# Even and odd dims of a head, gate and value weights in two loads, and an instruction order that is charged for changes of product kind

## The chip, the cores and the metric

The kernel runs on one core of a Trainium2 chip. The metric is device time in microseconds (us) of one execution. The profile is that of one execution; its span runs from the first to the last instruction of the program.

## The reference

Softcap attention, then a gated MLP, then a cosine MLP, all in float32 (the MLP weights come as float64):

```python
scores = cap * tanh((q @ k.T) / sqrt(64) / cap)       # 4 batches, 12 heads, 448 x 448
attn = exp(scores - max) / (sum + 1e-9);  o = attn @ v
x = o.transpose(0, 2, 1, 3).reshape(1792, 768)
y = (sigmoid(x @ w_gate) * (x @ w_val)) @ w_out        # 768 -> 1536 -> 768
h = y @ w_in2;  out = (h * cos(h)) @ w_out2            # 768 -> 2048 -> 768
```

## The kernel before, in words

**Planner.** The program is written by generators ("threads"), each of which yields one operation at a time (`Op`) with its engine, a cost in us, and what it reads and writes. `Order.run` (L184) keeps a planned time for each engine and, again and again, emits the thread whose operation can start earliest, after a penalty that the thread carries (L207). The order that comes out on each engine is the program; nothing is reordered on the chip. So a cost or a penalty changes no work, only the order. Two threads feed TensorE: `on_pe` of the attention, whose own sequence is fixed (L1535), and `whole` (L1770), which makes all other products. Until the key "late" is set they have penalties `ATT_PEN` (0.0) and `A_PEN` (0.5); after it `ATT_PE2` (0.5) and `A_PEN` (0.5), until the attention's last scores are out. "late" is set when the attention reaches step `W_FROM` (L1542); a step is half a group, and it also lets the loads of the gate and value weights begin (L563).

**Attention.** 12 groups of 4 heads of one batch; groups 0 to 5 make the first half of the tokens (x0), 6 to 11 the second (x1). A group has 8 scores steps (L1453: 2 heads at once, 6 matmuls of 448 columns over 64 rows), 8 values steps (L1482: 4 heads at once, each into its own 32 columns of the array; one step makes 32 of the 64 dims of each head), one step of sums (L1510, the same shape as a values step), and 4 transposes steps (L1429). ScalarE makes tanh and exp of every scores step. The reciprocal and the division (L1715, L1736) are VectorE's. Tiles of probabilities (`p`) lie in the 5 big buffers, as long as more than `P_BIG` are free, else in two small ones. They are freed by the values steps.

**Gate and value, first half.** 24 units of 128 columns of `w_gate` and `w_val`. A unit is loaded as raw float64 into a big buffer (`raw_load`, L438), converted to float32 by bit operations (`convert`: two on ScalarE, four on VectorE), kept in HBM for the second half (L493), split into a high and a low part (L519 ScalarE, L530 VectorE or GpSimd), and used for 6 product steps of 6 matmuls of 448 columns (L744). The rows of x0 in tile 2j + s are dims s * 32 to s * 32 + 31 of the four heads of group j, so a unit's rows are gathered by 8 transfers of 32 partitions (4 heads by 2 halves, `by_heads`, L413). At most one raw unit is on its way while the attention runs, two after. The units of the cosine MLP are loaded and converted in the background, one each `BG_STEP` us of the plan from `BG_FROM` on.

**After that.** The result of the first half (L744), gate and value of the second half in pairs of units (L756), its result (L744), and the cosine MLP of both halves (L756, L1297). TensorE runs these phases one after the other.

Of the kernel before, what the change touches and what calls it, by code (L numbers as in the profile page):

```python
# [9 lines left out]
I32 = mybir.dt.int32  # L10
# [111 lines left out]


class Op:
    __slots__ = ("forms", "reads", "writes", "size")

    def __init__(self, forms, reads, writes, size=0):
        self.forms, self.reads, self.writes, self.size = forms, reads, writes, size


class Thread:
# [5 lines left out]
class Order:  # L137
    LAT = 0.12
    AGE = 0.1
    DMA_LAT, DMA_RATE = 1.9, 230e3  # L140

    def __init__(self):
        self.free = dict.fromkeys(("PE", "ACT", "DVE", "POOL", "SP"), 0.0)
        self.port = self.dma = 0.0
        self.threads = []
        self.log = []

# [3 lines left out]
    def place(self, op):  # L151
# [11 lines left out]
                best = (t + cost + bias, t, form)  # L163
        return best[1], best[2]

    def emit(self, op, t, form):
        eng, cost, lock, fn, _ = form
        end = t + cost
        self.free[eng] = end
        if lock:  # L170
            self.port = end
        if eng == "SP":
            end = max(self.dma, t + self.DMA_LAT) + op.size / self.DMA_RATE
            self.dma = max(self.dma, t) + op.size / self.DMA_RATE
        for c in op.reads:
            if end > c.r:
                c.r, c.re = end, eng if eng != "SP" else None
        for c in op.writes:
            c.w, c.we = end, eng if eng != "SP" else None
            c.ok = True  # L180
        self.log.append((eng, t, t + cost, fn))
        fn()

    def run(self):  # L184
        while self.threads:
            best = None
            moved = True
            while moved:
                moved = False
                for th in list(self.threads):  # L190
                    if th.item is not None and not callable(th.item):
                        continue
                    if callable(th.item) and not th.item():
                        continue
                    try:
                        th.item = next(th.gen)
                        moved = True
                    except StopIteration:
                        self.threads.remove(th)
                        moved = True  # L200
            for th in self.threads:
                if callable(th.item) or not all(c.ok for c in th.item.reads):
                    continue
                t, form = self.place(th.item)
                if th.since is None:
                    th.since = t
                pen = (th.pen() if callable(th.pen) else th.pen) - self.AGE * (t - th.since)  # L207
                if best is None or t + pen < best[0]:
                    best = (t + pen, t, form, th)
            if best is None:  # L210
# [20 lines left out]
def pool_us(n):  # L231
    return 0.62 + n * 0.00173
# [6 lines left out]
def softcap_attention_gated_mlp_cos_mlp(  # L239
# [37 lines left out]
    H_PEN, S_PEN, H_STEP = -0.25, 0.2, 0.0  # L277
    LEAD, AHEAD = 99, 3
    BG_PEN, BG_RAW, BG_ROOM = 1.5, 2, 2
    BG_FROM, BG_STEP = 255.0, 14.5  # L280
    W_PEN, W_FROM = 0.3, 12
    ATT_PEN, A_PEN = 0.0, 0.5
    QK_PEN, SUM_PEN, DIV_PEN, XS_PEN = -1.0, -0.5, -2.0, 0.6
    SUM_BIAS, XH_BIAS, L_AHEAD = 0.3, 0.0, 4
    S_KEEP = (2, 1)
    TR_AT, DEN_AT = (3, 7), 5
    V_AT = ((), (0, 1, 2), (), (3,), (), (4, 5, 6), (), (7,))
    P_BIG = (0, 2)
    ATT_PE2, ATT_ACT2 = 0.5, 0.5
    G_SPARE = (1, 4)  # L290

    const = ctx.enter_context(tc.tile_pool(name="const", bufs=1))
    dram = ctx.enter_context(tc.tile_pool(name="dram", bufs=1, space=bass.MemoryType.DRAM))
# [35 lines left out]

    def pe(us, fn, r, w):
        return Op([("PE", us, False, fn, 0.0)], r, w)

    def act(n, fn, r, w, more=0.0):
        return Op([("ACT", act_us(n) + more, False, fn, 0.0)], r, w)
# [18 lines left out]
        )  # L355

    def dma(size, fn, r, w):
        return Op([("SP", 0.06, False, fn, 0.0)], r, w, size)

    W_A0, W_B0, W_A1, W_B1, W_CD = (7, 12), (7, 14), (13, 18), (7, 12), (12, 18)  # L360
    w_live = [0]
# [46 lines left out]

    def cols(w, k0, nk, c0, n):
        src = w[k0 * P : (k0 + nk) * P].bitcast(I32).rearrange("(k p) (f t) -> p k f t", p=P, t=2)  # L410
        return [(0, P, slice(0, nk), src[:, :, c0 : c0 + n, :])], nk, n

    def by_heads(w, c0, n):  # L413

        src = w.bitcast(I32).rearrange("(j h s d) (f t) -> h d j s f t", h=4, s=2, d=DQ, t=2)
        parts = [
            (h * DQ, DQ, slice(s, KD, 2), src[h, :, :, s, c0 : c0 + n, :]) for h in range(4) for s in range(2)
        ]
        return parts, KD, n

    for m in range(KF):
        units["g", m] = by_heads(w_gate, m * P, P)
# [13 lines left out]
    ykept_c = [Cell() for _ in range(KD)]  # L436

    def raw_load(u, b):  # L438
        parts, nk, n = units[u]
        t = b.ap[:, : 2 * UW].rearrange("p (k f t) -> p k f t", k=nk, t=2)  # L440
        for i, (p0, np_, ks, src) in enumerate(parts):
            yield dma(
                8 * UW * P // len(parts),
                lambda p0=p0, np_=np_, ks=ks, src=src: nc.sync.dma_start(out=t[p0 : p0 + np_, ks], in_=src),  # L444
                [],
                [b.cell(i)],
            )

    def convert(u, raw, f):
        pair = raw.ap[:, : 2 * UW].rearrange("p (f t) -> p f t", t=2)  # L450
        lo, hi = pair[..., 0], pair[..., 1]
        hf = hi.bitcast(F32)
        g = at(f, 0, UW)
        gi = g.bitcast(I32)
        rcs, fc = [raw.cell(i) for i in range(len(units[u][0]))], f.cell()
        yield act(UW, lambda: nc.scalar.activation(out=g, in_=hf, func=AF.Abs), rcs, [fc], 0.15)
        yield act(UW, lambda: nc.scalar.activation(out=hf, in_=hf, func=AF.Sign, bias=tiny), [], rcs, 0.15)
# [16 lines left out]
        yield dve(  # L474
            UW,
            lambda: nc.vector.scalar_tensor_tensor(  # L476
                out=gi, in0=lo, scalar=28, in1=gi, op0=ALU.logical_shift_right, op1=ALU.bitwise_or
            ),
            rcs,
            [fc],  # L480
        )
        yield dve(
            UW,
            lambda: nc.vector.scalar_tensor_tensor(  # L484
                out=gi, in0=gi, scalar=1, in1=hi, op0=ALU.logical_shift_right, op1=ALU.bitwise_xor
            ),
            rcs,
            [fc],
        )
        raw.free()  # L490
# [868 lines left out]
    def attention():  # L1359
# [58 lines left out]
        def transposes(g, s, part):  # L1418
# [11 lines left out]
                        b.ap[:, 0, c * CP : (c + 1) * CP], tv[:CP, c].rearrange("p h d -> p (h d)"), ident[:CP, :CP]  # L1430
                    )

            yield pe(0.46, fn, [t.cell(0), t.cell(1)], [b.cell()])
            t.free()
            tr[g, s, part] = b
            spawn(split_qk(g, s, part), QK_PEN, "split qk")
# [5 lines left out]
        def scores(g, kc):  # L1442
# [15 lines left out]
                            stop=(n_ == 2),  # L1458
                        )

            yield pe(0.69, fn, [x.cell(a) for x in (qs, ks) for a in "hl"], [b.cell()])
# [5 lines left out]
        def values(g, n_):  # L1467
# [11 lines left out]
            def fn():  # L1479
                for hh in range(4):  # L1480
                    s, h = divmod(hh, 2)
                    nc.tensor.matmul(  # L1482
                        ps(pv[x])[hh * DQ : (hh + 1) * DQ],
                        lhsT=vs[s][1][:CP, h, c, x * DQ : (x + 1) * DQ],
                        rhs=src[s].cols(c % 2, h)[:CP],
                        start=(c == 0),
                        stop=(c == NC - 1),
                    )

            yield pe(  # L1490
                0.75, fn, [t.cell() for t, _ in vs] + [p.cell(c % 2) for p in src], [pv[x].cell()]
            )
            if x:
                for p in src:
# [6 lines left out]
        def sums(g):  # L1501
# [13 lines left out]
                        stop=True,  # L1515
                    )

            yield pe(0.8, fn, [x.cell() for x in s_s], [den.cell()])
            for x in s_s:
                x.free()  # L1520
            spawn(divide(g, den), DIV_PEN, "divide")
# [38 lines left out]
        class Chunks:  # L1560
# [7 lines left out]
            def at(self, j, o=0, n=2 * S):  # L1568
                return at(self.t[0], 2 * j * S + o, n) if len(self.t) == 1 else at(self.t[j], o, n)
# [99 lines left out]
        def split_x(kk, b, o, c):  # L1669
            if kk not in x0_part:  # L1670
# [4 lines left out]
            src = at(o, c * S, S)  # L1675
            yield Op(
                [
                    ("POOL", pool_us(S), True, lambda: nc.gpsimd.tensor_copy(out=at(x.h, b * S, S), in_=src), 0.0),
                    ("DVE", dve2_us(S), True, lambda: nc.vector.tensor_copy(out=at(x.h, b * S, S), in_=src), XH_BIAS),
                ],  # L1680
                [o.cell(c)],
# [170 lines left out]
```

## Time and profile before

| | us |
|---|---|
| median of 3 runs | 1190.29 |
| the 3 runs | 1188.14 to 1191.30 |
| the profiled execution | 1188.98 |
| its span | 1186.8 |
| TensorE matmul busy in the span | 1151.9 |
| VectorE busy | 888.3 |
| ScalarE busy | 686.9 |
| GpSimd busy | 241.6 |

Matmuls are pipelined, so the busy time of one overlaps that of the next; what a step costs is read from start to start. A row of the timeline merges equal instructions that follow one another; in brackets stands the idle time ahead of the row and what ended it. L12 is line 12 of the kernel.

### The profile page before, as it was taken

The page shows a single profiled execution, that of the slowest core. Times are in us where ns is not written, and L with a number is a line of the kernel's source. Part 1 is how long each engine was busy: PE and PEld are TensorE (multiplying, and loading weights), DVE is VectorE, ACT ScalarE, POOL GpSimd, SP SyncE. Part 2 cuts the span into 40 slices and gives each one's busy share as a digit, 9 for nine tenths or more (in the row PEclk, how much of TensorE's full clock was granted, in tenths as well). Part 3 has the DMA queues.
Part 4 walks back from the last instruction along what each step waited for, and adds up shares of the span by engine and source line. Part 5 has one row for each costly group of instructions (what it writes and reads, how often), then busy time and mean ns, then how long its engine had stood idle before and what let it go on. Part 6 is the DMA issues. An engine that isn't in the chain of part 4 may idle for free.

```text
span 1186.8 us, 17008 instructions
## 1 busy us (share of the span) xinstructions
PE 1151.9 (97%) x6480; PEld 975.4 (82%) x6480; DVE 888.3 (75%) x1121; ACT 686.9 (58%) x813; POOL 241.6 (20%) x134
## 2 busy tenths in 40 slices
PE   8999989999997999999999999999999999999998
PEld 4444466566776989999999899999999999999998
DVE  5776868676849997788778886787779878586862
ACT  6888977768436645544445554676348337552720
POOL 2665521023002000023223000201213121021200
PEclk9999999999999999999999999999999999999999
DMA  7432364635647956653224572314115232111303
GB/s 182 101 79 74 90 162 128 161 99 161 182 142 222 316 183 223 208 181 98 94 93 133 170 261 87 109 42 144 40 43 199 65 110 79 54 54 40 93 2 93
DMA packets 128881, 148.25 MB, mean 125 GB/s; under 512 B 52640, under 2 KB 101664, under 8 KB 128800
## 3 DMA queue, kind: packets, MB, share of 16 engines
q1 hardware_dynamic: 128512, 147.10, 41.4%
q8 instruction: 51, 0.84, 0.3%
q14 instruction: 30, 0.25, 0.1%
q10 hardware_dynamic: 288, 0.07, 0.0%
HBM read 112.13 MB, written 35.00 MB: 124 GB/s over the span
## 4 chain that ended last, share of the span: by engine, by line
PE 89%; DVE 6%; ACT 2%; SPq 1%; issue 1%; DMA 1%; DVEq 0%; ACTq 0%
PE pt L756 29%; PE pt L744 27%; PE pt L1297 20%; PE pt L1482 6%; PE pt L1453 4%; DVE r L1715 2%; PE pt L1429 1%; SPq L444 1%; PE pt L1510 1%; DVE gl L981 1%; ACT p L1593 1%; ACT p L1611 1%; PE pt L1427 0%; DVE f L476 0%; DVE f L484 0%
## 5 line engine op out<-in xcount | busy, mean ns | idle before, releaser
L756 PE MATMUL pt<-x,wh 128*128 128x448 f32 (+1 forms) x1265 | 338.5, 364 | 0.0
L756 PEld LDWEIGHTS pt<-x,wh 128*128 128x128 f32 x1265 | 237.6, 188 | 18.5
L756 PE MATMUL pt<-x,wl 128*128 128x448 f32 x504 | 184.2, 366 | 0.0
L519 ACT CAST wh<-f 128x768 fp32r<-128x768 f32 (+1 forms) x164 | 123.1, 776 | 96.2 <-DVE f L684 81.1
L530 POOL TENSOR_TENSOR wl<-f,wh 128x768 fp32r<-128x768 f32 x43 | 88.5, 2060 | 359.1 <-ACT wh L519 302.3
L1297 PE MATMUL pt<-wh,zl 128*128 128x384 f32 x448 | 149.8, 334 | 0.2 <-DVE zl L1234 0.2
L1297 PE MATMUL pt<-wh,zh 128*128 128x384 f32 x448 | 149.7, 334 | 0.0
L1297 PE MATMUL pt<-wl,zh 128*128 128x384 f32 x448 | 149.7, 334 | 0.0
L1593 ACT ACTIVATE p<-pt,tanh_scale 112x896 f32<-112x896 f32 x96 | 92.5, 1007 | 41.3 <-PE pt L1453 39.4
L530 DVE TENSOR_TENSOR wl<-f,wh 128x768 fp32r<-128x768 f32 x93 | 95.8, 1035 | 20.9 <-ACT wh L519 16.8
L756 PEld LDWEIGHTS pt<-x,wl 128*128 128x128 f32 x504 | 94.7, 188 | 7.4
L744 PE MATMUL pt<-xh,wh 128*128 128x448 f32 x288 | 90.6, 395 | 7.6 <-ACT sg L1013 5.2
L1320 DVE TENSOR_TENSOR acc<-pt,acc 128x384 f32<-128x384 f32 x84 | 45.7, 553 | 59.6 <-PE pt L1297 59.4
L1611 ACT ACTIVATE p<-p,cap_sb 112x896 f32<-112x896 f32 (+1 forms) x68 | 89.9, 1351 | 0.1
L1482 PE MATMUL pt<-p,v 112*32 112x448 f32 x768 | 87.6, 557 | 0.8 <-ACT p L1611 0.8
L744 PEld LDWEIGHTS pt<-xh,wh 128*128 128x128 f32 x288 | 49.9, 191 | 43.4 <-issue 29.7
L1297 PEld LDWEIGHTS pt<-wh,zl 128*128 128x128 f32 x448 | 84.1, 188 | 0.5 <-DVE zl L1234 0.5
L1297 PEld LDWEIGHTS pt<-wl,zh 128*128 128x128 f32 x448 | 84.1, 188 | 0.1
L1297 PEld LDWEIGHTS pt<-wh,zh 128*128 128x128 f32 x448 | 84.1, 188 | 0.1
L744 PE MATMUL pt<-xl,wh 128*128 128x448 f32 x288 | 83.2, 370 | 0.0
L744 PE MATMUL pt<-xh,wl 128*128 128x448 f32 x288 | 83.2, 370 | 0.0
L1453 PEld LDWEIGHTS pt<-qs,ks 64*112 64x112 f32 x576 | 46.5, 171 | 44.1 <-issue 13.3
(127 smaller groups left out, 2038.7 us busy)
## 6 DMA issues: line engine op xcount, KB each, us to landing
f<-kept SPq DMA_DIRECT2D x100, 384.0 KB, 3.5
kept<-f SPq DMA_DIRECT2D x36, 384.0 KB, 2.9
braw<-in_moe_w_in_dram SPq DMA_DIRECT2D x16, 768.0 KB, 5.7
kept<-bf SPq DMA_DIRECT2D x32, 384.0 KB, 3.1
braw<-in_moe_w_out_dram SPq DMA_DIRECT2D x16, 768.0 KB, 6.2
raw<-in_moe_w_gate_dram SPq DMA_DIRECT2D x96, 96.0 KB, 3.3
raw<-in_moe_w_val_dram SPq DMA_DIRECT2D x96, 96.0 KB, 3.0
raw<-in_moe_w_out_dram SPq DMA_DIRECT2D x12, 768.0 KB, 6.5
```

Source lines behind the costliest of these rows:

```text
L444: lambda p0=p0, np_=np_, ks=ks, src=src: nc.sync.dma_start(out=t[p0 : p0 + np_, ks], in_=src),
L519: yield act(n, lambda: nc.scalar.copy(out=at(h, 0, n), in_=at(src, o, n)), sc, [h.cell("h")])
L530: lambda e: e.tensor_tensor(out=w.part(1, 0, n), in0=at(src, o, n), in1=w.part(0, 0, n).bitcast(F32), op=ALU.subtract),
L744: nc.tensor.matmul(b.ap[:, c, s0:s1], lhsT=w.part(wi, kk * P, P), rhs=x.part(xi, c * S + s0, s1 - s0), start=(first and (wi, xi) == (0, 0) ...
L756: nc.tensor.matmul(b.ap[:, c, s0:s1], lhsT=w.part(wi, o, P), rhs=x[xi][:, s0:s1], start=(first and (wi, xi) == (0, 0)), stop=(last and (wi ...
L1297: nc.tensor.matmul(b.ap[:, 0, :NB], lhsT=at(z[zi], t * P, P), rhs=w.part(wi, k * NB, NB), start=(first and (zi, wi) == (0, 0)), stop=(last ...
L1320: lambda: nc.vector.tensor_tensor(out=o, in0=ps(b, 0, NB), in1=o, op=ALU.add),
L1453: nc.tensor.matmul(ps(b, h)[:CP], lhsT=at(ks, ki * S + c * CP, CP)[r], rhs=at(qs, qi * S, S)[r], start=(n_ == 0), stop=(n_ == 2),)
L1482: nc.tensor.matmul(ps(pv[x])[hh * DQ : (hh + 1) * DQ], lhsT=vs[s][1][:CP, h, c, x * DQ : (x + 1) * DQ], rhs=src[s].cols(c % 2, h)[:CP], st ...
L1593: lambda: nc.scalar.activation(out=two(p.at(j))[:CP], in_=both(b)[:CP], func=AF.Tanh, scale=tanh_scale[:CP]),
L1611: lambda: nc.scalar.activation(out=pv, in_=pv, func=AF.Exp, scale=cap_sb[:CP]),
L1715: [("DVE", 2.95, False, lambda: nc.vector.reciprocal(out=at(r, 0, S), in_=ps(den)), 0.0)],
```

## The change

Four things. First, a values step now takes the even or the odd dims of each head instead of the lower or upper half, and the rows of the gate and value units are taken to match: row 256 j + 2 p + s goes to partition p, tile 2j + s. Second, such a unit is therefore loaded in 2 transfers of 128 partitions instead of 8 of 32. Third, the planner knows a kind of each TensorE operation (m: products, s: scores, v: values and sums, t: transposes) and adds a cost `ENTER` when the kind changes; the same amount times `STAY` is also a penalty in the choice of what comes next. Fourth, costs and parameters of the planner are set anew: a transfer's issue 0.42 us instead of 0.06, GpSimd's copy of 448 columns 0.57 us, TensorE's steps somewhat less; the loads of the weights may begin one group earlier (`W_FROM`), the attention's two threads get a penalty of -0.5 in place of 0.5 after "late", and `P_BIG`, `G_SPARE`, `QK_PEN`, `BG_FROM` and `BG_STEP` change.

```diff
+    ENTER = {"m": 0.19, "s": 0.19, "v": 0.12, "t": 0.15}
+    STAY = 1.0
...
+    def enter(self, op):
+
+        return self.ENTER[op.kind] if op.kind not in (None, self.kind) else 0.0
+
     def emit(self, op, t, form):
         eng, cost, lock, fn, _ = form
+        cost += self.enter(op)
+        self.kind = op.kind or self.kind
...
                 pen = (th.pen() if callable(th.pen) else th.pen) - self.AGE * (t - th.since)
+                pen += self.STAY * self.enter(th.item)
...
-    BG_FROM, BG_STEP = 255.0, 14.5
-    W_PEN, W_FROM = 0.3, 12
-    ATT_PEN, A_PEN = 0.0, 0.5
-    QK_PEN, SUM_PEN, DIV_PEN, XS_PEN = -1.0, -0.5, -2.0, 0.6
+    BG_FROM, BG_STEP = 270.0, 13.5
+    W_PEN, W_FROM = 0.3, 10
+    ATT_PEN, A_PEN = -0.5, 0.5
+    QK_PEN, SUM_PEN, DIV_PEN, XS_PEN = 0.0, -0.5, -2.0, 0.6
...
-    P_BIG = (0, 2)
-    ATT_PE2, ATT_ACT2 = 0.5, 0.5
-    G_SPARE = (1, 4)
+    P_BIG = (0, 1)
+    ATT_PE2, ATT_ACT2 = -0.5, -0.5
+    G_SPARE = (1, 6)
...
-        return Op([("SP", 0.06, False, fn, 0.0)], r, w, size)
+        return Op([("SP", 0.42, False, fn, 0.0)], r, w, size)
...
-        src = w.bitcast(I32).rearrange("(j h s d) (f t) -> h d j s f t", h=4, s=2, d=DQ, t=2)
-        parts = [
-            (h * DQ, DQ, slice(s, KD, 2), src[h, :, :, s, c0 : c0 + n, :]) for h in range(4) for s in range(2)
-        ]
-        return parts, KD, n
+        src = w.bitcast(I32).rearrange("(j p s) f -> p j s f", p=P, s=2)
+        return src[:, :, :, 2 * c0 : 2 * (c0 + n)], KD, n
...
+        t = b.ap[:, : 2 * UW].rearrange("p (j s f) -> p j s f", s=2, f=2 * n)
+        for s in range(2):
             yield dma(
-                8 * UW * P // len(parts),
-                lambda p0=p0, np_=np_, ks=ks, src=src: nc.sync.dma_start(out=t[p0 : p0 + np_, ks], in_=src),
+                4 * UW * P,
+                lambda s=s: nc.sync.dma_start(out=t[:, :, s], in_=src[:, :, s]),
                 [],
-                [b.cell(i)],
+                [b.cell(s)],
             )
...
-            yield pe(0.46, fn, [t.cell(0), t.cell(1)], [b.cell()])
+            yield pe(0.39, fn, [t.cell(0), t.cell(1)], [b.cell()], "t")
...
-                        lhsT=vs[s][1][:CP, h, c, x * DQ : (x + 1) * DQ],
+                        lhsT=vs[s][1][:CP, h, c, x::2],
...
-                    ("POOL", pool_us(S), True, lambda: nc.gpsimd.tensor_copy(out=at(x.h, b * S, S), in_=src), 0.0),
+                    ("POOL", 0.57, True, lambda: nc.gpsimd.tensor_copy(out=at(x.h, b * S, S), in_=src), 0.0),
```

## Rows read from the trace of the kernel before

**Rows 1.** The page's first part: busy time, share of the span, instructions.

```profile
PE 1151.9 (97%) x6480; PEld 975.4 (82%) x6480; DVE 888.3 (75%) x1121; ACT 686.9 (58%) x813; POOL 241.6 (20%) x134
```

**Rows 2.** Windows: stretch, length, busy (instructions) of each engine, TensorE clock, DMA share, GB/s.

```profile
core 0: us, PE busy (x) PEld busy (x) DVE busy (x) ACT busy (x) POOL busy (x), PEclk, DMA share, GB/s
107.00:155.00 48.00, 41.56 (x352) 19.74 (x348) 35.62 (x42) 42.05 (x44) 26.35 (x14) 0.96 0.45 111
...
290.00:375.00 85.00, 77.38 (x393) 61.60 (x392) 59.45 (x65) 42.67 (x49) 14.94 (x6) 0.98 0.62 175
375.00:411.00 36.00, 36.00 (x176) 32.69 (x176) 34.85 (x45) 21.74 (x25) 2.48 (x1) 1.00 0.83 276
...
430.00:1187.00 757.00, 751.25 (x3903) 712.47 (x3901) 570.64 (x741) 380.31 (x502) 114.97 (x64) 1.00 0.35 112
```

**Rows 3.** Timeline of TensorE while it makes attention alone: start, length, what.

```profile
117.10 0.94 PE L1510 MATMUL pt<-sum,ones 112*32 112x448 f32 x8
...
121.14 0.60 PE L1429 MATMUL pt<-ident,qk 112*128 112x112 f32 x4 [1.16 <-DVE r L1715]
...
129.58 1.48 PE L1453 MATMUL pt<-qs,ks 64*112 64x448 f32 x12
130.98 2.46 PE L1482 MATMUL pt<-p,v 112*32 112x448 f32 x24
133.26 0.94 PE L1510 MATMUL pt<-sum,ones 112*32 112x448 f32 x8
...
153.42 1.83 PE L1453 MATMUL pt<-qs,ks 64*112 64x448 f32 x11 [2.69 <-DVE r L1715]
```

**Rows 4.** Timeline of TensorE where attention and products alternate, and products in a row.

```profile
185.08 0.86 PE L1453 MATMUL pt<-qs,ks 64*112 64x448 f32 x6
185.88 0.68 PE L744 MATMUL pt<-xh,wh 128*128 128x448 f32 x2
...
187.30 0.96 PE L1482 MATMUL pt<-p,v 112*32 112x448 f32 x8
...
189.60 0.96 PE L1482 MATMUL pt<-p,v 112*32 112x448 f32 x8
...
290.87 0.57 PE L744 MATMUL pt<-xh,wh 128*128 128x448 f32 x2
...
292.11 0.57 PE L744 MATMUL pt<-xh,wh 128*128 128x448 f32 x2
```

**Rows 5.** Windows, line L1453 alone, then line L1482 alone, on TensorE.

```profile
155.00:357.00 202.00, 20.54 (x145) 0.99 0.54 147
...
155.00:357.00 202.00, 31.23 (x264) 0.99 0.54 147
```

**Rows 6.** The DMA queue's waits (total, times, longest), then timelines of TensorE and ScalarE.

```profile
SPq L444 <- PE pt L1482: 36.5, 3, 15.7
...
348.12 0.96 PE L1482 MATMUL pt<-p,v 112*32 112x448 f32 x8
...
355.16 0.93 ACT L456 ACTIVATE f<-raw 128x768 f32<-128x768 f32 x1 [12.81 <-DMA kept<-f]
...
363.02 1.12 PE L744 MATMUL pt<-xh,wh 128*128 128x448 f32 x2 [5.22 <-ACT sg L1013]
...
374.50 0.47 PE L744 MATMUL pt<-xh,wh 128*128 128x448 f32 x1 [2.40 <-DVE r L1715]
```

**Rows 7.** Timeline of the DMA queue: issues of raw units.

```profile
353.35 3.78 SPq L444 DMA_DIRECT2D raw<-in_moe_w_gate_dram  x8
...
368.90 0.39 SPq L444 DMA_DIRECT2D raw<-in_moe_w_out_dram  x1
```

**Rows 8.** Timeline of GpSimd: last low part of x0, low part of weight unit 0.

```profile
141.19 1.14 POOL L1686 TENSOR_TENSOR xl<-o,xh 128x448 fp32r<-128x448 f32 x1
...
150.88 1.80 POOL L530 TENSOR_TENSOR wl<-f,wh 128x768 fp32r<-128x768 f32 x1
```

**Rows 9.** The weight loads of L1482: shortest, median, longest in ns, first and last start.

```profile
L1482 PEld LDWEIGHTS pt<-p,v x768: 106/109/178, 21.2 to 348.2; 112*32 112x32 f32 x192
```

More of the change, by code (lines that the diff above doesn't have):

```diff
@@ L124, with __init__ @@
 class Op:
-    __slots__ = ("forms", "reads", "writes", "size")
-    def __init__(self, forms, reads, writes, size=0):
-        self.forms, self.reads, self.writes, self.size = forms, reads, writes, size
+    __slots__ = ("forms", "reads", "writes", "size", "kind")
+    def __init__(self, forms, reads, writes, size=0, kind=None):
+        self.forms, self.reads, self.writes, self.size, self.kind = forms, reads, writes, size, kind
 class Thread:
@@ L144, in __init__ @@
         self.port = self.dma = 0.0
+        self.kind = None
         self.threads = []
@@ L328, in softcap_attention_gated_mlp_cos_mlp, with pe @@
     spawn = sch.spawn
-    def pe(us, fn, r, w):
-        return Op([("PE", us, False, fn, 0.0)], r, w)
+    def pe(us, fn, r, w, kind="m"):
+        return Op([("PE", us, False, fn, 0.0)], r, w, kind=kind)
     def act(n, fn, r, w, more=0.0):
@@ L410, in cols @@
         src = w[k0 * P : (k0 + nk) * P].bitcast(I32).rearrange("(k p) (f t) -> p k f t", p=P, t=2)
-        return [(0, P, slice(0, nk), src[:, :, c0 : c0 + n, :])], nk, n
+        return src[:, :, c0 : c0 + n, :], nk, n
     def by_heads(w, c0, n):
-        src = w.bitcast(I32).rearrange("(j h s d) (f t) -> h d j s f t", h=4, s=2, d=DQ, t=2)
-        parts = [
-            (h * DQ, DQ, slice(s, KD, 2), src[h, :, :, s, c0 : c0 + n, :]) for h in range(4) for s in range(2)
-        ]
-        return parts, KD, n
+        src = w.bitcast(I32).rearrange("(j p s) f -> p j s f", p=P, s=2)
+        return src[:, :, :, 2 * c0 : 2 * (c0 + n)], KD, n
     for m in range(KF):
@@ L438, in raw_load @@
     def raw_load(u, b):
-        parts, nk, n = units[u]
-        t = b.ap[:, : 2 * UW].rearrange("p (k f t) -> p k f t", k=nk, t=2)
-        for i, (p0, np_, ks, src) in enumerate(parts):
+        src, nk, n = units[u]
+        if u[0] not in "gv":
+            t = b.ap[:, : 2 * UW].rearrange("p (k f t) -> p k f t", k=nk, t=2)
+            yield dma(8 * UW * P, lambda: nc.sync.dma_start(out=t, in_=src), [], [b.cell(0), b.cell(1)])
+            return
+        t = b.ap[:, : 2 * UW].rearrange("p (j s f) -> p j s f", s=2, f=2 * n)
+        for s in range(2):
             yield dma(
-                8 * UW * P // len(parts),
-                lambda p0=p0, np_=np_, ks=ks, src=src: nc.sync.dma_start(out=t[p0 : p0 + np_, ks], in_=src),
+                4 * UW * P,
+                lambda s=s: nc.sync.dma_start(out=t[:, :, s], in_=src[:, :, s]),
                 [],
-                [b.cell(i)],
+                [b.cell(s)],
             )
@@ L454, in convert @@
         gi = g.bitcast(I32)
-        rcs, fc = [raw.cell(i) for i in range(len(units[u][0]))], f.cell()
-        yield act(UW, lambda: nc.scalar.activation(out=g, in_=hf, func=AF.Abs), rcs, [fc], 0.15)
-        yield act(UW, lambda: nc.scalar.activation(out=hf, in_=hf, func=AF.Sign, bias=tiny), [], rcs, 0.15)
+        rc, r1, fc = raw.cell(0), raw.cell(1), f.cell()
+        yield act(UW, lambda: nc.scalar.activation(out=g, in_=hf, func=AF.Abs), [rc, r1], [fc], 0.15)
+        yield act(UW, lambda: nc.scalar.activation(out=hf, in_=hf, func=AF.Sign, bias=tiny), [], [rc, r1], 0.15)
         yield dve2(
@@ L478, in convert @@
             ),
-            rcs,
+            [rc],
             [fc],
@@ L486, in convert @@
             ),
-            rcs,
+            [rc],
             [fc],
@@ L1459, in fn @@
                         )
-            yield pe(0.69, fn, [x.cell(a) for x in (qs, ks) for a in "hl"], [b.cell()])
+            yield pe(0.605, fn, [x.cell(a) for x in (qs, ks) for a in "hl"], [b.cell()], "s")
             sc[g, kc] = b
@@ L1490, in values @@
             yield pe(
-                0.75, fn, [t.cell() for t, _ in vs] + [p.cell(c % 2) for p in src], [pv[x].cell()]
+                0.74, fn, [t.cell() for t, _ in vs] + [p.cell(c % 2) for p in src], [pv[x].cell()], "v"
             )
@@ L1516, in fn @@
                     )
-            yield pe(0.8, fn, [x.cell() for x in s_s], [den.cell()])
+            yield pe(0.74, fn, [x.cell() for x in s_s], [den.cell()], "v")
             for x in s_s:
```

## Prediction

> **What bounds the kernel now.** I read the page's first part first. TensorE's matmuls are busy 97% of the span, 1151.9 of 1186.8 us [rows 1], VectorE 75%, so TensorE is the engine to look at, and by this row only 34.9 us are idle. The windows then say where: from 430 us on TensorE is busy 751.25 of 757 us [rows 2]. Nothing there is touched by the change, except that everything would come earlier. What can be won lies ahead of that, so I went through the timeline of TensorE there and counted from start to start, since busy times of neighbours overlap.
>
> While attention runs alone, a group takes 16.16 us, from the sums at 117.10 to those at 133.26. Three values steps take 133.26 - 130.98 = 2.28 us, 0.76 each; two scores steps and the change to values take 1.40 us [rows 3]. Where attention and products alternate, a scores step and its change take 185.88 - 185.08 = 0.80, so the second scores step of the 1.40 is worth 0.60. A product step in a row with its like takes 292.11 - 290.87 = 1.24 us. Scores plus product plus both changes take 187.30 - 185.08 = 2.22, that is 0.38 more than 0.60 + 1.24; values plus product take 2.30, that is 0.30 more than 0.76 + 1.24 [rows 4]. These 0.30 to 0.38 us are no idle time in any row, and yet they are time that TensorE loses at each excursion from products to attention.
>
> The Trainium skill says in Perfetto Trace Analysis, section Identifying the Most-Contended Engine, that matmul busy time is no good measure of what is left, since matmuls are pipelined. The rows above agree: by busy time the excursions would cost nothing, the term for them below would be 0, and the sum would be -10.1 instead of -13.9 us.
>
> The last large loss is a stall. TensorE waits 5.22 us for a sigmoid until 363.02 and 2.40 us for a reciprocal until 374.50; the window 290 to 375 shows 77.38 busy of 85 us and a mean clock of 0.98 [rows 2, 6]. Both levels of the clock are in that mean: the first two products after the wait took 1.12 us where two usually take 0.57 [rows 4, 6]. Back from there: ScalarE had idled 12.81 us before it could begin to convert a raw weight at 355.16, and the DMA queue's raw loads waited for values steps three times, up to 15.7 us [rows 6]. That is a buffer: probabilities lie in big buffers, raw units need one, and the last group's values steps came one for each product unit, until 348.12, because after "late" both threads of TensorE had the same penalty.
>
> **The change part by part.**
>
> *The stall.* With -0.5 against 0.5 the attention's steps are emitted as soon as they can start, so the last group's values steps no longer lie between products, and the big buffers come free when its exps are done. I take the whole stall off: 5.22 + 2.40 + 1.5 for the half clock (a mean of 0.98 over 85 us is at most 1.7) = -9.1 us. Its bounds are 0, if the wait only moves, and -9.1.
>
> *Changes of kind.* Before, the stretch from 155 to 357 us has 145 / 6 = 24 scores steps and 264 / 8 = 33 values steps [rows 5]. At 0.38 and 0.30 that is 19.0 us; a few stand two or three in a row, so 18. After, these three groups (24 / 8) run nearly as in attention alone. A group's work there is 8 x 0.60 + 9 x 0.76 + 4 transposes at the plan's 0.39 = 13.2, and 16.16 - 13.2 - 1.16 (the wait for the reciprocal, [rows 3]) leaves 1.8 for its ten changes: 5.4 for three groups. The products now only fill what attention leaves open for over some 0.8 us (penalties 0.5 + 0.5, less 0.19 for the change back). I expect one visit for each pair of scores steps, four a group, over the 6.5 groups from the new "late" on: 26 x 0.34 = 8.8. Sum: -18 + 5.4 + 8.8 = -3.8. Bounds: -12.6 with no visits at all, +3 with twice as many visits.
>
> *An earlier start.* The first product begins at about 155 us. x0 was whole at 142.3 (141.19 + 1.14), weight unit 0 at 152.7 (150.88 + 1.80), so the weight was late, not x0 [rows 8]. `W_FROM` 10 begins its load a group, about 16 us, earlier, and the first two thirds of x0 are there sooner still. From 107 to 155 TensorE has 6.44 us idle in 48 [rows 2], among it 1.16 a group and 2.69 at 153.42 [rows 3]. Products can fill the later part: -4, bounds 0 and -6.4.
>
> *Two loads instead of eight.* Eight issues take 3.78 us of the DMA queue, one large one 0.39 [rows 7]; so 24 units save 24 x (3.78 - 0.78) = 72 us of the queue. The queue runs beside everything else; its cover is the raw unit loaded ahead. What it gives on the path is inside the stall's term. The real issue time and the plan's 0.42 now agree, where 0.06 made the plan believe that loads behind others came sooner. 0 by itself. Without its cover, a load would reach a waiting TensorE up to 3 us sooner.
>
> *Values with a stride.* The weight load of a values step now takes every second element. No row shows such a load. The plain one takes 0.109 us [rows 9] and lies beside the matmuls of the step before, which fill 0.76 us for two lots of four loads [rows 3], so it could become three times as long and stay hidden, except at the first of a run: with four runs a group and twice the time, 48 x 0.11 = +5. Below, nothing excludes 0; I take 0, as for the plain load. The Trainium skill, SBUF — State Buffer, section Door 1: The DMA port swizzle, says that reads keep full rate with at least two hits on each 16-byte line; every second float32 gives two, which would be 0 too, and no run here shows it.
>
> *The rest.* `QK_PEN`, `P_BIG`, `G_SPARE`, the background's times and GpSimd's cheaper copies only move work between engines with room or later in time. The background's first conversions go from 255 to 270 us of the plan, out of the way of the gate and value units. 0, but see the second rival.
>
> *A new wait.* Once the attention is out of the way, products run solid and a unit lasts 6 x 1.24 = 7.4 us, with VectorE converting at its limit: in 375 to 411 us TensorE is full, and VectorE is busy 34.85 of 36 us [rows 2]. This stretch now starts earlier and lasts some 150 us. I charge +3 for waits for weights, between 0 and +22 (below).
>
> Sum: -9.1 - 3.8 - 4 + 3 = -13.9 us. The profiled execution took 1188.98, so 1175.1; the median of the runs is 1.3 above it, so 1176.
>
> **The rivals.**
>
> *More comes out.* No visits (-12.6), all idle time of 107 to 155 filled (-6.4), no new wait: 9.1 + 12.6 + 6.4 = 28.1, so 1162. The unfilled waits for reciprocals and ScalarE (42.05 of 48 us busy, [rows 2]) speak against it: visits and filling exclude one another.
>
> *The stall stays.* `P_BIG` now lets late groups take a big buffer with only two free instead of three, so raw loads may wait for a big buffer as before, earlier. Then only -4.8 is left: 1185.5. For it speaks that three waits of this sort are in the trace [rows 6]; against it, that values steps now follow their exps at once.
>
> *The weights become the bound: slower.* With the attention first on ScalarE too (-0.5 against 0.3 for conversions), few units are ready when it ends, and from then on TensorE takes one each 7.4 us. VectorE is at 97% there already [rows 2]. If it needs 15% more than TensorE's time, over 150 us, that is +22 instead of +3: 1188.98 + 5.1 + 1.3 = 1195. It decides from about 14%, where the gain of 16.9 is used up and 3.6 more. Against it: GpSimd, busy 2.48 of 36 us there, can take low parts, and the background starts later.
>
> **How the numbers follow.** What this measurement can tell from no change is about 0.3%, 3.6 us: under 1186.7 is faster, over 1193.9 slower. The forecast, 1168 to 1184, has a chance of 0.57; more comes out, 0.12; the stall stays, 0.15, two thirds of it under 1186.7 and a third within; the weights become the bound, 0.16, of which 0.12 are over 1193.9 and the rest within. A slow strided load or more visits can lift any case by 3 to 5. So faster 0.77, same 0.10, slower 0.13. The range 1162 to 1194 leaves out about 2 in 10: half of the slow case and some of the best.
>
> **What would show it.** Right: the timeline of TensorE after about 230 us has products alone; no row idle over 3 us between 340 and 380; products first appear before 145 us; from 107 us to the end of attention no more than some 30 rows of products between attention's; the window from 430 us on is as full as before. Raw issues in rows of two, under 1 us. Wrong: TensorE rows that wait for L519, L530 or a sigmoid after the attention's end; a raw load that waits for L1482 over 5 us; values steps in a row of over 0.80 us each, which would be the stride.

## The result, and the profile after

The changed kernel takes 1158.37 us (median of 4 runs, 1155.79 to 1159.11) against 1189.22 (4 runs, 1187.27 to 1191.30). The ratio is 0.9736, with a 95% interval of 0.9712 to 0.9761: 31 us less, where 13 to 14 had been forecast, and under the lower end of the range, 1162.

The first part of the page of the changed kernel answers to [rows 1]. TensorE's busy time fell by 16.8 us, though its work is the same; the span fell by 30.6.

```profile
span 1156.2 us, 16726 instructions
...
PE 1135.1 (98%) x6480; PEld 979.2 (85%) x6480; DVE 892.0 (77%) x1130; ACT 674.0 (58%) x800; POOL 222.7 (19%) x125
```

The windows of the changed kernel, with columns as in [rows 2]:

```profile
0.00:107.00 107.00, 98.18 (x826) 50.06 (x830) 79.73 (x104) 91.52 (x84) 52.82 (x35) 1.00 0.51 121
107.00:155.00 48.00, 42.68 (x388) 20.61 (x380) 41.84 (x49) 44.32 (x44) 25.35 (x13) 1.00 0.41 109
155.00:226.00 71.00, 68.83 (x521) 36.55 (x520) 48.28 (x53) 56.13 (x54) 21.01 (x10) 1.00 0.27 81
226.00:382.00 156.00, 156.00 (x771) 144.60 (x771) 134.46 (x167) 92.70 (x107) 5.86 (x3) 1.00 0.75 240
382.00:470.00 88.00, 88.00 (x436) 81.57 (x435) 72.32 (x102) 48.92 (x64) 0.55 (x1) 1.00 0.63 215
```

The stretches before 290 us of the kernel before that [rows 2] don't hold, in the same view:

```profile
0.00:107.00 107.00, 95.53 (x810) 48.67 (x812) 73.41 (x97) 88.94 (x79) 59.46 (x38) 1.00 0.44 107
...
155.00:290.00 135.00, 133.41 (x777) 85.61 (x777) 96.04 (x111) 100.62 (x103) 23.37 (x11) 0.99 0.53 141
```

In this execution of the changed kernel TensorE has no gap from 226 us until the result phase is over, and the granted clock is 1.00 in all the windows. Before it was 0.96 from 107 to 155 and 0.98 from 290 to 375 [rows 2], and 0.99 between. These means hide three stretches at the lower of the clock's two levels (1.2 of 2.4 GHz), each begun in a wait of TensorE or within 2 us behind one (waits of 1.31, 2.69 and 5.22 us). Windows around them in the kernel before, with a mean clock of 0.57, so that each costs 0.43 x 4 = 1.7 us:

```profile
113.00:117.00 4.00, 4.00 (x25) 1.22 (x28) 0.00 (x0) 4.00 (x6) 2.71 (x2) 0.57 0.43 123
154.00:158.00 4.00, 4.00 (x17) 3.12 (x14) 2.39 (x3) 3.66 (x3) 0.00 (x0) 0.57 1.08 253
362.00:366.00 4.00, 2.98 (x8) 2.69 (x9) 3.86 (x6) 4.00 (x6) 0.40 (x1) 0.57 1.08 232
```

The timeline of TensorE in the changed kernel, where the products first appear, and at the end of the attention:

```profile
155.03 0.87 PE L1464 MATMUL pt<-qs,ks 64*112 64x448 f32 x6
155.83 0.67 PE L755 MATMUL pt<-xh,wh 128*128 128x448 f32 x2
...
218.82 6.22 PE L1493 MATMUL pt<-p,v 112*32 112x448 f32 x64
224.86 0.94 PE L1521 MATMUL pt<-sum,ones 112*32 112x448 f32 x8
225.73 0.67 PE L755 MATMUL pt<-xh,wh 128*128 128x448 f32 x2
```

The last group's eight values steps now stand in one row, 6.04 us from start to start, 0.76 each, and the sums follow at once. Before they came one for each product unit until 348.12 [rows 6]. The first product is no earlier: 155.83 against 155.18. The load of its raw weight unit is earlier: it is issued at 84.49 instead of 102.56. But the four steps of its conversion on VectorE are spread from 115.11 to 140.10, between the attention's, and its low part is done at 151.32, where it was done at 152.68 before [rows 8]. The issue and the low part:

```profile
84.49 0.94 SPq L455 DMA_DIRECT2D raw<-in_moe_w_gate_dram  x2
```

```profile
148.60 2.72 POOL L541 TENSOR_TENSOR wl<-f,wh 128x768 fp32r<-128x768 f32 x1 [1.15 <-ACT wh L530]
```

The end of gate and value, in the same view, first before and then after:

```profile
411.19 0.57 PE L744 MATMUL pt<-xh,wl 128*128 128x448 f32 x2
411.60 0.57 PE L744 MATMUL pt<-gh,wh 128*128 128x448 f32 x2
```

```profile
382.28 0.57 PE L755 MATMUL pt<-xh,wl 128*128 128x448 f32 x2
382.69 0.57 PE L755 MATMUL pt<-gh,wh 128*128 128x448 f32 x2
```

So 28.9 of the 30.6 us are won by here. The result phase after it takes 87.5 us instead of 90.5, and what follows 1.3 more.

### The profile page after: what moved, and what is told of

It reads as the page before. It is cut to its first block, busy times and chain, and to the rows that moved or that the text cites. A ratio compares the mean times of both kernels' runs of the same rounds, so it can differ in the third digit from the quotient of the medians.

```text
span 1156.2 us, 16726 instructions
## 1 busy us (share of the span) xinstructions
PE 1135.1 (98%) x6480; PEld 979.2 (85%) x6480; DVE 892.0 (77%) x1130; ACT 674.0 (58%) x800; POOL 222.7 (19%) x125
## 4 chain that ended last, share of the span: by engine, by line
PE 94%; DVE 3%; ACT 2%; issue 1%; DVEq 0%; ACTq 0%
PE pt L767 31%; PE pt L755 30%; PE pt L1308 20%; PE pt L1493 6%; PE pt L1464 4%; PE pt L1440 1%; DVE r L1726 1%; ACT p L1604 1%; ACT p L1622 1%; PE pt L1521 1%; PE pt L1438 0%; DVE sum L1669 0%; DVE ks L1710 0%; DVE qs L1710 0%; DVE sg L948 0%
## 5 line engine op out<-in xcount | busy, mean ns | idle before, releaser
L541 POOL TENSOR_TENSOR wl<-f,wh 128x768 fp32r<-128x768 f32 x40 | 81.8, 2047 | 349.4 <-ACT wh L530 200.2
L1622 ACT ACTIVATE p<-p,cap_sb 112x1792 f32<-112x1792 f32 (+1 forms) x63 | 88.7, 1435 | 0.0
L1493 PE MATMUL pt<-p,v 112*32 112x448 f32 x768 | 82.6, 545 | 1.7 <-DVE qs L1714 0.9
L755 PE MATMUL pt<-xh,wh 128*128 128x448 f32 x288 | 83.1, 370 | 0.0
L755 PE MATMUL pt<-gl,wh 128*128 128x448 f32 (+1 forms) x277 | 78.9, 366 | 0.7 <-DVE gl L992 0.7
```

The lines of the kernel that those rows point to most:

```text
L541: lambda e: e.tensor_tensor(out=w.part(1, 0, n), in0=at(src, o, n), in1=w.part(0, 0, n).bitcast(F32), op=ALU.subtract),
L755: nc.tensor.matmul(b.ap[:, c, s0:s1], lhsT=w.part(wi, kk * P, P), rhs=x.part(xi, c * S + s0, s1 - s0), start=(first and (wi, xi) == (0, 0) ...
L1493: nc.tensor.matmul(ps(pv[x])[hh * DQ : (hh + 1) * DQ], lhsT=vs[s][1][:CP, h, c, x::2], rhs=src[s].cols(c % 2, h)[:CP], start=(c == 0), sto ...
L1622: lambda: nc.scalar.activation(out=pv, in_=pv, func=AF.Exp, scale=cap_sb[:CP]),
```

## The experiments

Two figures tell the runs apart: when the last matmul of gate and value starts, and how long the result phase lasts from there. Both are read from the timeline of TensorE in each run's one profiled execution, while the median and the ratio are those of all its executions. The passes are those from an attention step to a product in each program's order. The intervals of e10, e11 and e12 overlap that of the changed kernel, so what is said of these three rests on their traces.

| | median, us | ratio (95%) | gate and value end | result phase | passes |
|---|---|---|---|---|---|
| before | 1189.22 | 1 | 411.4 | 90.5 | 64 |
| changed | 1158.37 | 0.9736 (0.9712 to 0.9761) | 382.5 | 87.5 | 13 |
| e1 precedence alone | 1173.12 | 0.985 (0.981 to 0.989) | 386.3 | 100.1 | 8 |
| e2 two loads alone | 1179.17 | 0.9907 (0.9875 to 0.994) | 396.1 | 93.3 | 64 |
| e3 changed, no charge | 1167.53 | 0.9807 (0.9774 to 0.9839) | 383.1 | 92.3 | 15 |
| e4 changed, old parameters | 1169.28 | 0.9838 (0.9798 to 0.9879) | 395.6 | 91.4 | 46 |
| e5 changed, eight loads | 1171.66 | 0.9837 (0.9805 to 0.987) | 387.8 | 95.3 | 9 |
| e6 precedence and two loads | 1172.50 | 0.9855 (0.9808 to 0.9903) | 387.1 | 96.2 | 8 |
| e7 changed, background early | 1166.04 | 0.9792 (0.9758 to 0.9825) | 381.8 | 94.8 | 13 |
| e9 changed, start late | 1157.10 | 0.9721 (0.9684 to 0.9758) | 378.9 | 92.0 | 12 |
| e10 changed, start early | 1163.22 | 0.9772 (0.9739 to 0.9804) | 387.0 | 87.6 | 21 |
| e11 changed, background late | 1161.65 | 0.9759 (0.9727 to 0.9791) | 383.4 | 90.9 | 13 |
| e12 changed, old issue cost | 1161.20 | 0.9762 (0.9728 to 0.9796) | 381.9 | 91.6 | 11 |
| e13 precedence, low parts sooner | 1159.75 | 0.9756 (0.9724 to 0.9788) | 385.7 | 87.6 | 8 |
| e14 start late, low parts sooner | 1153.81 | 0.9702 (0.9678 to 0.9725) | 379.6 | 87.6 | 12 |
| e15 as e14, sooner still | 1153.44 | 0.9702 (0.9678 to 0.9725) | 378.1 | 87.6 | 12 |

**Which part makes the gain.** Four kernels, each with one part alone or one taken out.

e1, on the kernel before:

```diff
-    ATT_PE2, ATT_ACT2 = 0.5, 0.5
+    ATT_PE2, ATT_ACT2 = -0.5, -0.5
```

> The kernel before with one line changed: both penalties of the attention after its 'late' key are -0.5 instead of 0.5; nothing else. Theory A (the attention's precedence makes the gain: it ends excursions between products and the stall): 1160 to 1168 us, product pace 0.2027 us per matmul once the attention is over. Rival B (the charge for changes of kind makes it): 1183 to 1190. Rival C (loads in two pieces make it, the pace among it): 1183 to 1190, pace 0.2065 as long as units come in 8 pieces.

1173.12 us. Two numbers in one line bring 25.1 of the 28.9 us up to the end of gate and value. But the result phase takes some 9.5 us longer than before. Theory A is right on the first stage and misses the total by 5 us. The waits of TensorE in e1 from 226 to 480 us, and then the window in which they lie:

```profile
PE pt L744 <- DVE gl L981: 7.3, 2, 4.8
```

```profile
386.00:412.00 26.00, 18.66 (x77) 16.13 (x76) 25.31 (x32) 13.48 (x18) 2.22 (x1) 0.81 0.51 166
```

TensorE waits twice for a low part of gate times value (`gl`), is busy 18.66 of 26 us, and gets a mean clock of 0.81, a mixture of both levels (1.00 up to 402 us, 0.51 after it); VectorE is busy 25.31 of 26.

e2, on the kernel before: the even and odd dims with two loads a unit, and nothing else.

```diff
-        src = w.bitcast(I32).rearrange("(j h s d) (f t) -> h d j s f t", h=4, s=2, d=DQ, t=2)
+        src = w.bitcast(I32).rearrange("(j p s) f -> p j s f", p=P, s=2)
...
+        for s in range(2):
+                lambda s=s: nc.sync.dma_start(out=t[:, :, s], in_=src[:, :, s]),
...
-                        lhsT=vs[s][1][:CP, h, c, x * DQ : (x + 1) * DQ],
+                        lhsT=vs[s][1][:CP, h, c, x::2],
```

> The kernel before with even and odd dims and two loads a unit, nothing of the planner. The same order on TensorE. Theory A and rival B: 1186 to 1191, the stall of some 8 us between 355 and 375 us stays. Rival C: 1160 to 1172, and pace 0.2027 in place of 0.2065 between 290 and 425 us. If the strided weight load costs something, values steps in a row take over 0.76 us.

1179.17 us, faster than theory A and rival B said, and not as fast as C said. The program has as many passes as before, 64, and yet the stall is gone; the window from 290 to 375 us, which had 77.38 us busy in [rows 2], shows:

```profile
290.00:375.00 85.00, 85.00 (x445) 70.44 (x444) 72.79 (x88) 47.16 (x54) 11.50 (x5) 1.00 0.71 232
```

Its queue issued the last raw unit of gate and value at 340.09, in two. The kernel before issued three from 349.14 on, each in eight (the one between the two shown is in [rows 7]):

```profile
340.09 0.93 SPq L445 DMA_DIRECT2D raw<-in_moe_w_val_dram  x2
```

```profile
349.14 3.64 SPq L444 DMA_DIRECT2D raw<-in_moe_w_val_dram  x8
...
358.66 9.66 SPq L444 DMA_DIRECT2D raw<-in_moe_w_val_dram  x8
```

So at 332 us the queue of e2 had one unit left to issue, that of the kernel before three. Before, the queue then stood 15.7 us for a values step, until 349.14; in e2 it waits for values steps no longer than 2.6 us from 300 us on, though they still lie between products, up to 343 us. e2 also prices the strided load. Its weight loads of values, against [rows 9]:

```profile
L1483 PEld LDWEIGHTS pt<-p,v x768: 106/110/114, 20.7 to 343.2; 112*32 112x32 f32 x192
```

The median is 110 ns against 109: taking every second element costs 1 ns at most. The Trainium skill, SBUF — State Buffer, section Door 1: The DMA port swizzle, says that full rate needs at least two hits on each 16-byte line, and every second float32 gives two; this row agrees with it.

e3, on the changed kernel, without the charge:

```diff
-    ENTER = {"m": 0.19, "s": 0.19, "v": 0.12, "t": 0.15}
+    ENTER = {"m": 0.0, "s": 0.0, "v": 0.0, "t": 0.0}
```

> The changed kernel with all four charges for changes of kind at 0. Theory A: 1156 to 1163, since the attention's precedence stays. Rival B: 1175 to 1190. Rival C: 1156 to 1163.

1167.53 us: 9 us are lost, more than theory A allowed and less than B asked. They are not lost where kinds change. There are 15 passes instead of 13, and gate and value end 0.6 us later. The result phase takes 4.8 us longer, with one wait of 2.8 us for `gl` and 1.7 us lost at the lower clock after it. The profiled execution was the shortest of four, 1164.05 us; the rest of the 9 us is in no trace.

e4, on the changed kernel, with the seven lines of parameters of before:

```diff
-    BG_FROM, BG_STEP = 270.0, 13.5
-    W_PEN, W_FROM = 0.3, 10
-    ATT_PEN, A_PEN = -0.5, 0.5
-    QK_PEN, SUM_PEN, DIV_PEN, XS_PEN = 0.0, -0.5, -2.0, 0.6
+    BG_FROM, BG_STEP = 255.0, 14.5
+    W_PEN, W_FROM = 0.3, 12
+    ATT_PEN, A_PEN = 0.0, 0.5
+    QK_PEN, SUM_PEN, DIV_PEN, XS_PEN = -1.0, -0.5, -2.0, 0.6
...
-    P_BIG = (0, 1)
-    ATT_PE2, ATT_ACT2 = -0.5, -0.5
-    G_SPARE = (1, 6)
+    P_BIG = (0, 2)
+    ATT_PE2, ATT_ACT2 = 0.5, 0.5
+    G_SPARE = (1, 4)
```

> The changed kernel with every penalty and time of before (only charges, costs and the two loads are new). Theory A: 1176 to 1190, because the two threads alternate again. Rival B: 1158 to 1168. Rival C: 1160 to 1175.

1169.28 us, better than A said, short of B and inside C's range. It is 9.9 us under the two loads alone (e2, measured beside it), with 46 passes instead of 64. In the table its gate and value end only half a microsecond before those of e2, but that is the one execution that was profiled, at 1176.63 us, where the other three took 1167.97 to 1169.84. Its trace has TensorE at the lower clock from 22 to 26, 144 to 149 and 185 to 193 us, which costs 6.8 us against 1.7 in e2. So without the precedence, charges and costs together are likely worth something, fewer passes among it (the two intervals just touch); which of the two does it was not tried.

**Whether the parts add up, and what the result phase waits for.**

e5, the changed kernel with the halves and eight loads of before, so the edit of e2 undone:

```diff
-        src = w.bitcast(I32).rearrange("(j p s) f -> p j s f", p=P, s=2)
+        src = w.bitcast(I32).rearrange("(j h s d) (f t) -> h d j s f t", h=4, s=2, d=DQ, t=2)
...
-                        lhsT=vs[s][1][:CP, h, c, x::2],
+                        lhsT=vs[s][1][:CP, h, c, x * DQ : (x + 1) * DQ],
```

> The changed kernel with halves and eight loads of 32 partitions a unit again; planner as in the change. Theory A2 (the losses before the end of the gate and value phase can be ended by the precedence, by the loads or by the charges; each alone gets most of the same 29 us): that phase ends within 4 us of 382.5, total 1157 to 1166. Rival C2 (two loads are a needed part): it ends after 390, total over 1168. Pace: if eight-piece loads bring the pace of 0.2067, it is seen while gate and value units are loaded.

1171.66 us. Gate and value end at 387.8, between the two forecasts, and the total is the rival's. That end is not late for want of weights. Products run at the slower of two paces there (see the last section), worth some 3 us, and two stretches at the lower clock cost 3.4. The eight loads do not bring the slow pace, for e1 has eight as well and runs the same phase at the fast one. 7.8 us of the 13.3 are in the result phase, with 4.2 us of waits for `gl` and its high part.

e6, the kernel before with the edits of e1 and e2 together:

```diff
-    ATT_PE2, ATT_ACT2 = 0.5, 0.5
+    ATT_PE2, ATT_ACT2 = -0.5, -0.5
...
+        src = w.bitcast(I32).rearrange("(j p s) f -> p j s f", p=P, s=2)
...
+                        lhsT=vs[s][1][:CP, h, c, x::2],
```

> The kernel before with the attention's precedence (-0.5, -0.5) and the two loads, nothing else. Theory A2: gate and value end at 382 to 387, since both parts win the same time and don't add up; the result phase after it shows waits for VectorE (the low parts of gate times value) of 5 to 10 us as with the precedence alone; total 1162 to 1176. Rival (the parts add up: 18 + 12 us): under 1162.

1172.50 us: no better than e1. The parts don't add up, as A2 said. The traces of e1 and e2 show why, if what each wins up to the end of gate and value is split into idle time, time lost at the lower clock, the pace of products (some 2 us in both), and a rest that can only lie in changes of kind, since the work is the same:

| us won | all | idle | lower clock | pace | rest | passes |
|---|---|---|---|---|---|---|
| e1 precedence alone | 25.1 | 6.8 | 1.7 | 2 | 14.6 | 64 to 8 |
| e2 two loads alone | 15.3 | 8.8 | 3.4 | 2 | 1.1 | 64 to 64 |

With no pass less, the rest of e2 shows how far the reckoning can be off, 1 us. The loads win the stall and no changes of kind. The precedence wins the stall too, and the changes of kind besides, so the loads have nothing to add to it.

e7, the changed kernel with the background's times of before:

```diff
-    BG_FROM, BG_STEP = 270.0, 13.5
+    BG_FROM, BG_STEP = 255.0, 14.5
```

> The changed kernel with the background conversions' times of before (from 255, one each 14.5 us of the plan); same order on TensorE. Theory D (the later background is what keeps VectorE free for the result phase): waits of 5 us or more of TensorE for VectorE between 382 and 475 us, total 1162 to 1170. Rival: the other parameters or the charges keep them away: total within 3 us of 1158.

1166.04 us. Gate and value end as in the changed kernel (381.8), and TensorE then waits 4.4 us for `gl`. Theory D had said 5 or more; the place and the total are its.

e11, the other way:

```diff
-    BG_FROM, BG_STEP = 270.0, 13.5
+    BG_FROM, BG_STEP = 285.0, 13.0
```

> The changed kernel with the background conversions from 285 us of the plan, one each 13.0. Theory D (VectorE's room before the result phase decides): no wait of TensorE between 382 and 475 us, total 1155 to 1160. Rival (270 was just met, any other time brings waits back): 1161 to 1168.

1161.65 us, with waits of 2.7 us for `gl`. VectorE had more room, 130.81 us busy from 226 to 382 against 134.46 in the changed kernel, and theory D said no wait. It falls in this form: more room for VectorE is not what decides.

In e1, VectorE makes four steps of a weight's conversion from 398.58 to 401.70 and only then the low part that TensorE waits for until 402.84; its high part was done on ScalarE by 399.5. e13 leaves the work alone and changes its order, on the kernel of e1. The thread makes both parts, so the order on ScalarE moves too:

```diff
-            spawn(g_split(hf), 1.0, f"g{hf}")
+            spawn(g_split(hf), 0.0, f"g{hf}")
```

> The kernel before with the attention's precedence alone (as in e1), and the thread that splits gate times value into high and low parts with penalty 0.0 instead of 1.0. Theory E (the result phase waits because VectorE has these low parts behind conversions that are not urgent): no wait of over 1 us for the low parts between 386 and 412 us, no half clock there, total 1160 to 1167 against 1173.1. Rival F (VectorE has no room there whatever its order): TensorE then waits for weight parts instead, total 1169 to 1178.

1159.75 us. The same window as in e1:

```profile
386.00:412.00 26.00, 26.00 (x130) 24.10 (x129) 25.72 (x34) 17.43 (x24) 2.62 (x1) 1.00 0.64 218
```

VectorE is as busy as in e1, 25.72 of 26 us, and TensorE is full, at full clock. Theory E is right: not the room but the order. Two lines of the kernel before, this one and that of e1, bring it to within 1.4 us of the whole change (by the ratios 0.9756 and 0.9736, which are each taken beside the kernel before, within 2.4).

**The smaller terms.** Three edits, each alone, on the changed kernel. e9:

```diff
-    W_PEN, W_FROM = 0.3, 10
+    W_PEN, W_FROM = 0.3, 12
```

> The changed kernel with the weights' loads beginning at step 12, as before, instead of 10. The prediction's term for the earlier start was -4 us. If it holds: 1161 to 1164. Rival (the start is worth nothing, since the attention goes first and leaves no room before its end): within 3 us of 1158, first product after 160 us.

e10:

```diff
-    W_PEN, W_FROM = 0.3, 10
+    W_PEN, W_FROM = 0.3, 8
```

> The changed kernel with the weights' loads beginning at step 8, another group earlier. If an earlier start fills TensorE's waits during the attention: 1150 to 1156, first product before 135 us. Rival: more excursions (21 instead of 13) and conversions in the way of the attention on ScalarE cost as much: 1156 to 1165.

e12:

```diff
-        return Op([("SP", 0.42, False, fn, 0.0)], r, w, size)
+        return Op([("SP", 0.06, False, fn, 0.0)], r, w, size)
```

> The changed kernel with a transfer's issue planned at 0.06 us again instead of 0.42. If the honest cost is needed: waits for raw units come back, total 1163 to 1175. Rival (with two loads a unit the queue has room, so its price in the plan doesn't matter): within 4 us of 1158.

e9 takes 1157.10 us: starting the weights a group later costs nothing. Gate and value even end 3.6 us earlier, and the result phase gives that back with a wait of 2.3 us for `gl` and a mean clock of 0.92 from 378 to 400 us. e10 takes 1163.22, the rival's side: its first product stands at 124.73, but idle time up to the end of gate and value is only 0.7 us less than in the changed kernel, 15.6 against 16.3. There are 21 passes, the attention's last step begins 13 us later (238.2 against 225.3), and gate and value end 4.5 us later. e12 takes 1161.20, within the rival's 4 us, and the difference from the changed kernel is not clear of the noise.

**A version with a lower median.** e14, on the changed kernel; e15 is the same with -0.5 in place of the 0.0:

```diff
-    W_PEN, W_FROM = 0.3, 10
+    W_PEN, W_FROM = 0.3, 12
...
-            spawn(g_split(hf), 1.0, f"g{hf}")
+            spawn(g_split(hf), 0.0, f"g{hf}")
```

> The changed kernel with the weights' loads from step 12 (as in e9) and the split of gate times value at penalty 0.0. e9 had gate and value done 3.6 us before the changed kernel and gave it back in 3.5 us of waits for low parts and a half clock. Theory E: the waits go, 1151 to 1155. Rival F: 1156 to 1162.

> As the one before, with penalty -0.5. Theory E: 1151 to 1155, as with 0.0. Rival F: slower than with 0.0, 1157 to 1165, since weight parts come later.

1153.81 and 1153.44 us, with no wait of TensorE from 226 to 480 us in either. Their runs, 1152.94 to 1154.42, lie under all of the changed kernel's (1155.79 to 1159.11), though on other occasions; the intervals of the ratios, 0.9678 to 0.9725 and 0.9712 to 0.9761, still touch, so that it is the better of the two is likely and not shown.

**e8**, the changed kernel once more, is told in the last section.

## Why the prediction was wrong

The side and the place were right; the size was half. Two terms failed: changes of kind were priced at a third of their worth, and the earlier start at -4 for something that did not happen. Against the prediction's own terms, span to span, 30.6 us in all:

*The stall* was priced at -9.1 and is gone: 7.62 us of idle time and 1.7 at the lower clock, so the size was right. Why it would go was half right. The chain back to the big buffers stands in the rows: the queue's wait of 15.7 us ends at 349.14, as the values step of 348.12 does. The precedence ends the stall (e1), but so do the two loads, with values steps between products as before (e2). The prediction gave the loads 0 by themselves; e2 shows that alone they bring 15.3 us up to the end of gate and value, where the precedence is not there to win the stall first. Its sign against itself, a raw load that waits over 5 us for values steps, is in the changed kernel as well, and more of it in all than before [rows 6]:

```profile
SPq L455 <- PE pt L1493: 40.6, 6, 14.3
```

But all of these waits lie before 226 us, while the attention keeps TensorE busy, and there they do no harm that the trace shows. So the sign was badly chosen: it needed a time.

*Changes of kind* were priced at -3.8, and this is the term that was mis-sized. What the runs show for it is 11. Up to the end of gate and value 28.9 us are won. Idle time fell from 11.47 + 6.44 + 1.59 + 7.62 = 27.1 us to 8.82 + 5.32 + 2.17 = 16.3, so 10.8 less. The three stretches at the lower clock cost 5.1, and in this execution there is none after. A slower pace of products, for some 490 of them from 290 us on at 0.004 each, was worth about 2 (see the last section). That leaves 28.9 - 10.8 - 5.1 - 2 = 11.0. The working erred at both ends. It counted 57 steps and charged 18 us before, where 64 passes at its own 0.34 are 21.8; and it expected 26 visits after, where there are 13, worth 4.4. With some 27 changes more within the attention at its own 0.18, 4.9, the counts give 21.8 - 4.4 - 4.9 = 12.5, and the 11.0 agree within 2 us. In e1 the same counts give 56 x 0.34 - 26 x 0.18 = 14.4, and the rest in the table above is 14.6. So the price of one change held; the number of visits was a guess, and twice too high. (The upper bound of the term is also summed wrongly: with twice as many visits it is -12.6 + 17.6 = +5, not +3.)

Not all of the 28.9 is the change's for certain. In a second execution of the changed kernel (e8) one stretch at the lower clock, from 186 to 191 us, costs 1.7 us, and the pace, too, differs between executions of one program. Some 4 us of what the two profiles differ by can be luck of the executions taken.

*An earlier start* was priced at -4 for products that fill waits. That step fails. The load came 18 us earlier, but not the weight: its conversion, in between the attention's work, took until 151 us all the same. The prediction had seen that the weight was late, and took the load for the reason. A group less of lead loses nothing (e9), and a group more brings the first product to 124.73 and wins 0.7 us of idle time (e10). Idle time before 155 us did fall, by 11.47 + 6.44 - 8.82 - 5.32 = 3.8 us, but with attention alone. The 2.69 us wait at 153.42 [rows 3] is among what is gone; the causes of that were not tried one by one. That the sum of the term comes close is luck.

*A new wait* was priced at +3 and is 0. The third rival named the right engine and the wrong phase: while gate and value run, TensorE never waits for weights after 226 us, in no run. VectorE's backlog shows in the result phase, as waits for `gl`: 1.8 to 2.3 us in the kernel before, e2 and e4, and 2 to 7 us in e1, e3, e5, e6, e7, e9, e11 and e12, in all of these but e11 with a stretch at the lower clock beside them. The changed kernel has none there. That the order decides is shown on the kernel of e1 (e13) and of e9 (e14). The changed kernel's result phase is 3.0 us shorter than before, 2.2 of it such waits, which no term had.

The charge, which names the change, does little through what it charges once the precedence is there. Without it the passes are 15 instead of 13 (e3). What it is worth, some 9 us of which 4.8 are seen in the result phase, comes from another order; why just that order has no waits was not settled. Without the precedence it may do more (e4). `P_BIG`, `G_SPARE`, `QK_PEN` and the new costs of TensorE's steps were not tried one by one.

## What to carry to other kernels

Where a planner interleaves two streams on one engine, count the passes between them and price a pass from start to start: busy rows hide it. Parts of a change that each end the same stall don't add up, so take the sum over losses and not over edits. And when an earlier phase gets faster, look at what its consumers need first from the next engine: here, another order on a full engine was worth some 11 us by the ratios and 13 by the medians (e1 to e13), with no work removed. And read a wait together with its time: a wait of the queue that led to a stall when it ended at 349 us did no harm that a trace shows before 226.

## What the hardware showed

The same products run at two paces. In the timeline of the kernel before six take 292.11 - 290.87 = 1.24 us [rows 4]; in that of the changed kernel six take 346.21 - 344.99 = 1.22:

```profile
344.99 0.57 PE L755 MATMUL pt<-xh,wh 128*128 128x448 f32 x2
...
346.21 0.57 PE L755 MATMUL pt<-xh,wh 128*128 128x448 f32 x2
```

Over long stretches the means are 0.2067 and 0.2027 us a matmul, at a granted clock of 1.00 in both. The pace holds over hundreds of products. The kernel before runs slow from about 290 to 428 us.

> The changed kernel once more, for one look. Theory P (the pace of the products, 0.2027 or 0.2067 us, is set by chance at a wait and differs between executions of one program): the stretches at either pace lie otherwise than in the first profile. Rival (it belongs to the program): the slow pace begins at 633 us and nowhere else.

e8 took 1156.97 us and answers for the main part of theory P. In the first profile of this program the second half's result phase runs slow, six in 661.49 - 660.25 = 1.24 us; in the second, at the same place, fast, 661.69 - 660.47 = 1.22. First profile, then e8:

```profile
660.25 0.57 PE L755 MATMUL pt<-gh,wh 128*128 128x448 f32 x2
...
661.49 0.57 PE L755 MATMUL pt<-gh,wh 128*128 128x448 f32 x2
```

```profile
660.47 0.56 PE L755 MATMUL pt<-gh,wh 128*128 128x448 f32 x2
...
661.69 0.57 PE L755 MATMUL pt<-gh,wh 128*128 128x448 f32 x2
```

So it is not the program's. Over the 432 matmuls of such a phase it makes 432 x 0.004 = 1.7 us. That it is set at a wait is not shown: both executions have the same wait of 0.70 us there, at 628.37 and at 629.12, and in the first profile the pace turns at 632.1, 3.7 us behind the wait, in the midst of products. What sets it was not found.
